# Performer attention and a Fourier-mixing block on one core: keys and queries of 18 of 32 pairs turned by VectorE instead of TensorE, and the other transposes made as row halves

## The chip, the cores and the metric

The kernel runs on one core of a Trainium2 chip. The metric is the device time of one execution in microseconds (us). In the listings PE is TensorE's matmul, PEld its weight load, DVE is VectorE, ACT is ScalarE, POOL is GpSimd, and SP is SyncE, which here only issues DMAs.

## The reference

Two layers follow each other. The first is linear attention by random features (Performer), with B = 8, H = 8, S = 576, D = 64 and 128 features:

```python
scale = 1.0 / np.sqrt(np.sqrt(D))
def phi(x):                                   # x is q * scale or k * scale
    proj = np.einsum('bhsd,md->bhsm', x, omega)
    h = proj - np.sum(x * x, axis=-1, keepdims=True) / 2.0
    return np.exp(h - np.max(h, axis=-1, keepdims=True)) / np.sqrt(m)
kv = np.einsum('bhsm,bhsd->bhmd', k_p, v)     # k_p = phi(k), q_p = phi(q)
z = np.sum(k_p, axis=2)
out = np.einsum('bhsm,bhmd->bhsd', q_p, kv) / (np.einsum('bhsm,bhm->bhs', q_p, z)[..., None] + 1e-06)
```

Its result, with the heads side by side, is x (8, 576, 512). The second layer mixes it by Fourier transforms and applies a two-layer network to each token:

```python
mixed = np.real(np.fft.fft(np.fft.fft(x, axis=1), axis=2))
u = x + mixed
un = (u - mean(u)) / np.sqrt(var(u) + 1e-06)  # over the last axis
return u + np.maximum(un @ w_ch1, 0.0) @ w_ch2
```

w_ch1 is 512 x 2048 and w_ch2 2048 x 512. Both come as 64-bit floats; the kernel reads their two 32-bit words and makes 32-bit floats of them itself. All else is 32-bit float.

## The kernel before, in words

**Pairs.** The attention goes by 32 pairs of heads: pair n is batch n // 4 and two neighbouring heads, with 2 x 576 rows. A load (`loads`, L464) puts nine rows of one head on each of 128 partitions: partition 64 i + p holds rows 9 p to 9 p + 8 of head i, the keys as 9 x 64 numbers, and the queries of the same rows behind them, in one `kq` buffer. There are two such buffers. Keys and queries are one DMA each, in runs of 9 x 64 x 4 = 2,304 bytes; the values (`load_v`) go to buffers of 65 columns a row, in runs of 256 bytes.

The features need keys and queries with the 64 numbers of a head on the partitions. `transposed` (L590) makes that: a buffer's 18 x 64 columns are nine blocks of 128 x 128, and TensorE turns each against an identity (L607) into PSUM. Four blocks fill a bank (2 KB on each of the 128 partitions; there are eight), so the groups are blocks 0 to 3, 4 to 7, and 8. `evicted` (L611) copies each group to `kqT`, on VectorE (L621) or ScalarE (L623). Then `attn` (L668) multiplies by omega (L701: two 64-row matmuls at a time for the first six pairs, four 64 x 64 ones for the others), `softmax` (L637) takes the row maximum (L644, VectorE) and the exponential (L661, ScalarE), L735 makes `kv` with `z` as a 65th column, and a second call of `transposed` turns the query features into `qeT`, in the groups 0, 1 to 4 and 5 to 8, which `evicted` writes in a changed order of rows, two copies for each group. L782 and L790 multiply by kv, and VectorE divides: one reciprocal for each pair (L799, L800) and a multiplication, on VectorE (L811) or ScalarE (L807), which leaves the pair's part of x.

**Mixing.** When the four pairs of a batch are done, `mix` (L823) folds x by the symmetry of the cosine and sine tables (L838 to L874, on VectorE or POOL) and multiplies by the tables. `residual` (L980) then makes u: the cosine part A and the sine part B lie in PSUM; ScalarE copies B to `bmp` (L988), VectorE forms A - B and A + B from it (four products with a scalar, L993, and two sums, L996), x is added, and u goes to DRAM (L1020).

**Network.** The first four tiles of 128 tokens go through an ordinary network in the first part (`plain_norms`, `norm_of`, `plain`), which makes the norm, turns the tile on TensorE (L1172), and multiplies by w1 and w2. Meanwhile `weights` loads the 64-bit weights slab by slab and `narrow` (L522) converts each of 32 slabs: a scaling on ScalarE or POOL (L532), bit operations on VectorE, a product on VectorE (L544) and a sum (L550). The other 4,096 tokens go in eight blocks of 512 through a second part, in which both matrix products use two levels of a Strassen-like scheme (`halves`; L1727, L1878 and L2178 are its matmuls). Its input has to be normed, turned and stored. For twelve tiles of 128 tokens of blocks 1 to 3 that is done ahead, by `ahead` (L1573): four DMAs bring the tile into a borrowed buffer, ScalarE makes the two sums and the norm, POOL the deviation, VectorE turns it by 32 x 32 squares (L1608), and a DMA stores it.

**What sets the order.** All of this is written as Python generators of `Step`s. A step names its engine, or two with a duration each where there is a choice, what must have been made (`after`), and which buffers and PSUM banks it takes and gives ("bank" is one bank, "duo" two neighbouring ones). `Listing.run` (L272) puts the steps in one order, in which the instructions then stand on each engine; nothing reorders them later. The order is recorded: `PICKS` (first part) and `PICKS2` (second part) say for every step which stream comes next and which engine it gets, `BANKS` and `BANKS2` which bank. The twelve tiles ahead are not in these lists. `BETWEEN` and `BETWEEN2` name the points at which the next piece of one is put between listed steps, and `PLACES` the borrowed buffer of each:

```python
PLACES = "kkktttkktuuu"          # k: a kq buffer, t: a kqT/qeT buffer, u: one of its own
...
    if kind == "k":
        place = ld.tile([P, 2 * R, D], F32, name="kq", tag="kq")
```

## Time and profile before

| | |
|---|---|
| median of 3 runs | 1122.09 us (1121.17, 1122.09, 1122.16) |
| the profiled execution, its span from first to last instruction | 1119.2 us |
| instructions in the profile | 31,666, 12,467 of them matmuls and transposes on PE |
| matmul busy time | 1108.4 us of the span |
| VectorE, ScalarE, POOL busy time | 888.7, 539.5 and 390.6 us |
| moved by DMA | 236 MB: 182 read from and 56 written to HBM |

The views that the prediction shows are read in this way. The page's first lines give each engine's busy time with its share of the span and its count. The rows of tenths cut the span in 40 equal slices and give the busy share of each engine in tenths, and the clock that TensorE was granted. The chain of work that ended last is followed back from the last instruction, and its shares are by engine and by line; "banks" stands for all PSUM tiles. A row of a stretch has its start and end, its length, then for PE, PEld, DVE, ACT and POOL the busy time with the number of instructions, then the granted clock, the DMA engines' mean share and GB/s; where a stretch is asked for one line alone, only the engine of that line is listed. A group's row names line, engine, operation, destination and sources, shape and count, then its busy time, the mean of one instruction in ns, and the idle time in front of it with what ended that. A matmul's record holds its latency too, so records overlap.

### The profile page before, as it was taken

The numbers are of one execution on the slowest core, as the hardware profiler recorded it, in microseconds if no ns is written. First come the engines' busy times: TensorE is split into PE (matmuls) and PEld (weight loads), VectorE is DVE, ScalarE is ACT, GpSimd is POOL, SyncE is SP. The second block draws the span as 40 slices with busy tenths as digits, with TensorE's granted clock in tenths as the row PEclk, the third lists the DMA queues.
The fourth block names the chain that finished last, engine by engine and source line by source line (L and its number), as shares of the span: only waits on it lengthen the run. The fifth ranks groups of instructions, "written<-read, shape, count | busy, mean of one in ns | idle before, by whom it ended". The sixth has DMA issues, their size and how long they took to land.

```text
span 1119.2 us, 31666 instructions
## 1 busy us (share of the span) xinstructions
PE 1108.4 (99%) x12467; PEld 1000.4 (89%) x12467; DVE 888.7 (79%) x1685; ACT 539.5 (48%) x1644; POOL 390.6 (35%) x401
## 2 busy tenths in 40 slices
PE   9999999999999999999999999999999999999998
PEld 7888888879868778999999889999889999889998
DVE  6999999987576767687697777888677888568895
ACT  7998898856536455623214452223463223331221
POOL 2443443553563348634413464000365000152000
PEclk9999999999999999999999999999999999999999
DMA  8856766665674669798896778747678656546453
GB/s 243 243 174 188 242 180 191 183 208 176 216 232 156 194 172 343 224 314 262 260 326 224 226 216 248 207 148 238 206 207 261 207 155 216 170 152 220 146 160 105
DMA packets 196549, 236.13 MB, mean 211 GB/s; under 512 B 53808, under 2 KB 120624, under 8 KB 196400
## 3 DMA queue, kind: packets, MB, share of 16 engines
q1 hardware_dynamic: 195904, 233.83, 68.1%
q8 instruction: 99, 1.62, 0.6%
q14 instruction: 50, 0.41, 0.1%
q10 hardware_dynamic: 496, 0.26, 0.1%
HBM read 182.13 MB, written 56.10 MB: 213 GB/s over the span
## 4 chain that ended last, share of the span: by engine, by line
PE 92%; DVE 3%; ACT 2%; DMA 2%; issue 0%; POOL 0%; SPq 0%; DVEq 0%; ACTq 0%
PE banks L2178 31%; PE banks L1727 27%; PE banks L1236 5%; PE banks L701 5%; PE banks L607 5%; PE banks L1259 5%; PE banks L1878 4%; PE banks L735 3%; PE banks L782 2%; PE banks L944 2%; PE banks L894 1%; ACT e L661 1%; DVE nmx L644 1%; PE banks L904 1%; DMA unw<-turned 1%; DMA raw<-in_moe_w_ch_dram 1%
## 5 line engine op out<-in xcount | busy, mean ns | idle before, releaser
L2178 PE MATMUL banks<-wl,sums 128*128 128x128 f32 x1792 | 219.8, 275 | 0.0
L2178 PEld LDWEIGHTS banks<-wl,sums 128*128 128x128 f32 x1792 | 210.6, 192 | 1.0 <-issue 0.3
L661 ACT ACTIVATE e<-banks,nmx 128x128 f32<-128x128 f32 x576 | 165.7, 441 | 23.3 <-DVE nmx L644 22.9
L644 DVE TENSOR_REDUCE nmx<-banks 128x8 f32<-128x1024 f32 (+1 forms) x96 | 89.3, 951 | 16.8 <-PE banks L701 12.4
L2178 PE MATMUL banks<-wl,hid 128*128 128x128 f32 x768 | 99.2, 275 | 0.3 <-DVE part L2154 0.3
L2178 PEld LDWEIGHTS banks<-wl,hid 128*128 128x128 f32 x768 | 92.8, 192 | 1.2 <-DVE part L2154 0.8
L2149 ACT ACTIVATE s<-banks 128x128 f32<-128x128 f32 x112 | 30.9, 277 | 113.6 <-PE banks L2178 103.5
L1727 PE MATMUL banks<-unw,wxw 128*128 128x256 f32 x352 | 85.4, 379 | 0.0
L701 PE MATMUL banks<-om,kqT 64*64 64x128 f32 (+1 forms) x2088 | 79.0, 275 | 1.7 <-ACT kv L751 1.3
L701 PEld LDWEIGHTS banks<-om,kqT 64*64 64x64 f32 (+1 forms) x2088 | 64.5, 138 | 12.7 <-issue 3.2
L2178 PE MATMUL banks<-wl,hx 128*128 128x128 f32 x576 | 74.2, 275 | 0.4 <-DVE part L2154 0.4
L1727 PEld LDWEIGHTS banks<-unw,wxw 128*128 128x128 f32 x352 | 66.6, 190 | 8.9
L1727 PE MATMUL banks<-rx,wxw 128*128 128x256 f32 x288 | 70.8, 379 | 0.0
L2178 PEld LDWEIGHTS banks<-wl,hx 128*128 128x128 f32 x576 | 69.4, 192 | 0.8 <-DVE part L2154 0.6
L1752 ACT ACTIVATE s<-banks 128x512 f32<-128x512 f32 x65 | 38.5, 596 | 65.1 <-PE banks L1727 60.0
L1727 PE MATMUL banks<-ttw,wxw 128*128 128x256 f32 x288 | 69.8, 379 | 0.0
L1236 PE MATMUL banks<-unT,w 128*128 128x128 f32 x512 | 65.4, 279 | 1.7 <-DVE qeT L621 1.7
L550 POOL TENSOR_TENSOR w<-w,raw 128x512 f32<-128x512 f32 x28 | 37.6, 1351 | 77.3 <-DVE raw L544 68.1
L2227 POOL TENSOR_TENSOR more<-more,part 128x512 f32<-128x512 f32 x2 | 2.6, 1315 | 176.6 <-ACT part L2220 176.6
L1236 PEld LDWEIGHTS banks<-unT,w 128*128 128x128 f32 x512 | 60.2, 192 | 4.5 <-issue 2.3
L1727 PEld LDWEIGHTS banks<-rx,wxw 128*128 128x128 f32 x288 | 54.5, 190 | 7.3
L1727 PEld LDWEIGHTS banks<-ttw,wxw 128*128 128x128 f32 x288 | 54.5, 190 | 7.3
(287 smaller groups left out, 2442.3 us busy)
## 6 DMA issues: line engine op xcount, KB each, us to landing
wl<-w2l SPq DMA_DIRECT2D x245, 256.0 KB, 3.9
wxw<-w1x SPq DMA_DIRECT2D x120, 256.0 KB, 3.1
raw<-in_moe_w_ch_dram SPq DMA_DIRECT2D x32, 512.0 KB, 4.8
kq<-in_k_dram SPq DMA_DIRECT2D x32, 288.0 KB, 4.5
kq<-in_q_dram SPq DMA_DIRECT2D x32, 288.0 KB, 4.5
vd<-in_v_dram SPq DMA_DIRECT2D x32, 288.0 KB, 5.4
ur<-us SPq DMA_DIRECT2D x30, 256.0 KB, 5.2
w2l<-sums SPq DMA_DIRECT2D x14, 512.0 KB, 4.9
```

The source lines that it names most:

```text
L550: eng.tensor_tensor(out=dst, in0=dst, in1=lof, op=ALU.add)
L607: nc.tensor.transpose(ps[:, (j - j0) * 128 : (j - j0 + 1) * 128], src(j), ident[:])
L644: nc.vector.tensor_reduce(nmx[:, :, 0:num], pps[:, :, 0 : MF * num].rearrange("p b (c m) -> p b c m", m=MF), axis=AX.X, op=ALU.max, negate ...
L661: nc.scalar.activation(out=e[:, c + (i if num == 1 else 0), :], in_=pps[:, i, MF * c : MF * c + MF], func=AF.Exp, bias=nmx[:, i, c : c + 1],)
L701: nc.tensor.matmul(pps[cols, c, MF * m : MF * m + MF], lhsT=kqT[rows, j, cols], rhs=om2[rows, :],)
L735: nc.tensor.matmul(kvp[cols, i, 0 : D + 1], lhsT=feature(r)[rows, cols], rhs=vds[n % NV][rows, r, :], start=(r == 0), stop=(r == R - 1),)
L1236: nc.tensor.matmul(hp[:, 0:TP], lhsT=w1[:, dc, 128 * fc : 128 * fc + 128], rhs=unTs[key][:, dc, :], start=(dc == 0), stop=(dc == NDC - 1),)
L1259: nc.tensor.matmul(yp[:, 0:DM], lhsT=hs[fc][:, 128 * i : 128 * i + 128], rhs=w2[:, fc, :], start=(fc == 0), stop=(fc == NFC - 1),)
L1727: nc.tensor.matmul(ps[:, span * f : span * f + span].rearrange("f (b q) -> f b q", q=Q), lhsT=left[:, P * f : P * f + P], rhs=right, start ...
L1752: nc.scalar.activation(out=s[:], in_=ps, func=AF.Copy)
L1878: nc.tensor.matmul(cell.rearrange("f t (b q) -> f t b q", q=Q), lhsT=w[:, d, col : col + 128], rhs=right[:, :, d].rearrange("f (t b) q -> ...
L2178: nc.tensor.matmul(ps[:, 0:128], lhsT=left[:, f], rhs=wls[head(j), i, n][:, f], start=start and f == 0, stop=(f == 3), skip_group_check=True,)
```

## The change

**Loads and turns of pairs.** A constant `NTURN = 14` parts the pairs. For pairs 0 to 13, keys and queries are loaded into alternating 64-column places, so that a block of 128 columns holds keys and queries of the same rows; each run of a DMA is 256 bytes. For pairs 14 to 31, `load_blocks` brings keys and queries as squares of 32 x 32 numbers that already stand where they belong, two DMAs each for keys and queries, in runs of 128 bytes. VectorE's transpose, which turns each 32 x 32 square in its place, then makes `kqT` from the buffer in two instructions of 512 and 640 columns. These pairs have no TensorE transposes and no PSUM for `kqT`.

**Row halves.** The other transposes of the pairs, those of omega and those of the four plain tiles are made by `half_turned`: two matmuls on 64 rows each, one on the upper and one on the lower half of the array, each moving 64 columns into a bank of its own. A group then takes two banks and may have five blocks: 0 to 3 and 4 to 8 for `kqT`, 0 to 4 and 5 to 8 for `qeT`. The changed order of rows in `qeT` comes from the identity, which is now loaded from DRAM with a permutation in its other quarters, and from the order in which PSUM is written (`spaced`), so that `evicted` is one plain copy for each group.

**Other parts.** `residual` for all but a batch's last tile has ScalarE prepare A (the odd columns copied, the even ones with B's middle column added or subtracted), and VectorE makes A - B and A + B as two sums of 257 columns. The cosine and sine tables have their columns in order of frequency (even, then odd), and the matmul behind them writes every second column of PSUM. The product in `narrow` may go to POOL, as two instructions. The tiles ahead are listed steps: nine in the first part (`aheads`), three in the second. `wash`, six matmuls that open the second part, gives its banks back after "held". `PICKS` has three digits a step, and the four lists of order and banks are all new.

Counted over the program: 609 transposes of 128 x 128 become 894 of 64 rows; VectorE has 1,611 instructions (1,687 before), ScalarE 1,566 (1,593), POOL 429 (406), SP 1,078 (1,042).

```diff
+    NTURN = 14
     def loads():
         for n in range(B * NP):
             b, pr = divmod(n, NP)
             h = slice(2 * pr, 2 * pr + 2)
-            rows = "i (p r) d -> (i p) r d"
-            yield Step(SP, 0.37, 3.0, take=("kq",), makes=("k", n), kb=288)
+            yield Step(SP, 0.8, 3.6, take=("kq",), makes=("k", n), kb=288)
             kq = ld.tile([P, 2 * R, D], F32, name="kq", tag="kq")
-            nc.sync.dma_start(kq[:, 0:R, :], k[b, h].rearrange(rows, r=R))
             kqs[n] = kq
-            yield Step(SP, 0.47, 3.6, makes=("kq", n), kb=288, bias=-2.98)
-            nc.sync.dma_start(kq[:, R : 2 * R, :], q[b, h].rearrange(rows, r=R))
+            load_blocks(kq, 0, k[b, h], n < NTURN)
+            yield Step(SP, 0.8, 4.0, makes=("kq", n), kb=288, bias=-2.98)
+            load_blocks(kq, 1, q[b, h], n < NTURN)
+
+    def load_blocks(kq, c, src, whole):
+        if whole:
+            nc.sync.dma_start(kq[:, c::2, :], src.rearrange("i (p r) d -> (i p) r d", r=R))
+            return
+        src = src.rearrange("i s d -> (i s) d").rearrange("(a j r) d -> j r a d", j=Q, r=R)
+        dst = kq[:].rearrange("p c d -> p (c d)").rearrange("p (r a i) -> p r a i", r=R, i=Q)
+        for db in range(2):
+            rows = slice(D * c + Q * db, D * c + Q * db + Q)
+            nc.sync.dma_start(dst[rows], src[:, :, :, Q * db : Q * db + Q])
...
-    make_identity(nc, ident[:])
+    for r in range(2):
+        eyes[r, np.arange(D), r, np.arange(D)] = 1.0
+        eyes[r, turn_, 1 - r, np.arange(D)] = 1.0
+    nc.scalar.dma_start(ident[:], nc.inline_tensor(eyes.reshape(128, 128), name="k_eyes").ap())
...
-        yield Step(DVE, 0.61, give=("sign",), port=True, bias=-0.99)
+        step = Step({DVE: 0.61, POOL: 3.0}, give=("sign",), port=True, bias=-0.99)
...
+    def half_turned(to, src, turn=False):
+        for r in range(2):
+            rows, cols = slice(D * r, D * r + D), slice(D * (r ^ turn), D * (r ^ turn) + D)
+            nc.tensor.transpose(to(r), src[rows], ident[rows, cols])
+
+    def spaced(ps, r, at, c):
+        out = ps[:, r, :]
+        return bass.AP(out.tensor, out.offset + at + c, [list(out.ap[0]), [128, 2], [67 - 2 * c, 2], [4, 16]])
+
-    def transposed(src, name, groups, after, makes, give, order=None):
+    def transposed(src, name, groups, after, makes, give, mirror=False):
...
-                0.109 * m,
+                0.062 * m,
+                mode="rows",
                 after=after(j0, j1),
-                take=("bank",) + (("turned",) if j0 == 0 else ()),
+                take=("duo",) + (("turned",) if j0 == 0 else ()),
...
             for j in range(j0, j1):
-                nc.tensor.transpose(ps[:, (j - j0) * 128 : (j - j0 + 1) * 128], src(j), ident[:])
-            yield Fork(evicted(dst, b, j0, j1, makes, order))
+                i = j - j0
+                def to(r):
+                    if not mirror:
+                        return ps[:, r, D * i : D * i + D]
+                    if j == 0:
+                        return ps[:, r, 0:D].rearrange("q (s t) -> q t s", s=2)
+                    c = (j - 1) % 4
+                    return spaced(ps, r, D * (j - c - j0), c)
+                half_turned(to, src(j), mirror and j > 0)
+            yield Fork(evicted(dst, b, j0, j1, makes, mirror))
...
-        for i in range(s):
-            of = ps[:, i, :, ::-1, ::-1] if i and j0 else ps[:, i]
-            copy(dst[:, i], of)
+        if step.eng == DVE:
+            nc.vector.tensor_copy(out=dst, in_=ps)
+        else:
+            nc.scalar.activation(out=dst, in_=ps, func=AF.Copy)
...
+        else:
+            for j0, j1 in ((0, 4), (4, R)):
+                yield Step(
+                    DVE, 0.03 + 0.168 * (j1 - j0), after=(("kq", n),), take=("turned",) if j0 == 0 else (),
+                    give=("kq",) if j0 else (), makes=("kqT", n, j0),
+                )
+                if kqT is None:
+                    kqT = att.tile([128, R, 128], F32, name="kqT", tag="turned")
+                nc.vector.transpose(out=kqT[:, j0:j1, :], in_=flat[:, j0:j1, :])
...
-            ((0, 1), (1, 5), (5, R)),
+            ((0, 5), (5, R)),
...
-                    ab[p1 * n : p1 * n + np_, n, cols],
+                    ab[p1 * n : p1 * n + np_, n, m:KD:2],
...
+        if c < NL:
+            yield Step(ACT, 0.62, take=("bmp",), bias=0.1)
+            bmp, (aa, mi, pl) = taken()
+            nc.scalar.activation(out=mi[:, KD:], in_=pb[:, KD : KD + 1], func=AF.Copy)
+            nc.scalar.activation(out=pl[:, KD:], in_=pb[:, KD : KD + 1], func=AF.Copy, scale=-1.0)
+            nc.scalar.activation(out=aa[:, 1:KD:2], in_=pa[:, 1:KD:2], func=AF.Copy)
+            for k, mid in ((0, mi), (2, pl)):
+                nc.scalar.activation(out=aa[:, k:KD:4], in_=pa[:, k:KD:4], func=AF.Identity, bias=mid[:, KD:])
+            for last, (dst, op) in enumerate(((mi, ALU.subtract), (pl, ALU.add))):
+                yield Step(DVE, 0.34, give=(b0, b1) if last else (), bias=-0.1)
+                nc.vector.tensor_tensor(out=dst[:, 0:KD], in0=aa[:, 0:KD], in1=pb[:, 0:KD], op=op)
...
-    def ahead(j, i):
+    def ahead(j, i, name, pool):
...
+    PLACED = ("kq", "kq", "kq", "turned", "turned", "turned", "kq", "kq", "turned")
+    def aheads():
+        yield Step(NONE, after=tuple(("x", B - 1, pr) for pr in range(NP)))
+        for m, name in enumerate(PLACED):
+            j, i = divmod(m, TB // 128)
+            yield Fork(ahead(1 + j, i, name, ld if name == "kq" else att), 500.0)
...
-        yield Step(NONE, give=(b,))
+        yield Step(NONE, after=("held",), give=(b,))
```

426 lines of the change are left out of this document (255 added, 171 removed).

## The prediction

> **What bounds the kernel now.** I read the page first (engines, tenths, the chain that ended last), then stretches of the span, then the groups of instructions by line and shape, then the DMA rows.
>
> ```profile
> span 1119.2 us, 31666 instructions
> PE 1108.4 (99%) x12467; PEld 1000.4 (89%) x12467; DVE 888.7 (79%) x1685; ACT 539.5 (48%) x1644; POOL 390.6 (35%) x401
> PE   9999999999999999999999999999999999999998
> DVE  6999999987576767687697777888677888568895
> PEclk9999999999999999999999999999999999999999
> ...
> PE 92%; DVE 3%; ACT 2%; DMA 2%; issue 0%; POOL 0%; SPq 0%; DVEq 0%; ACTq 0%
> PE banks L2178 31%; PE banks L1727 27%; PE banks L1236 5%; PE banks L701 5%; PE banks L607 5%; PE banks L1259 5%; PE banks L1878 4%; PE banks L735 3%; PE banks L782 2%; PE banks L944 2%; PE banks L894 1%; ACT e L661 1%; DVE nmx L644 1%; PE banks L904 1%; DMA unw<-turned 1%; DMA raw<-in_moe_w_ch_dram 1%
> ```
>
> The reader is to see that PE is never idle by the record, at full clock (PEclk), and that 92% of the chain is PE. But a matmul's record holds its latency as well as its turn, so "99% busy" leaves room, and DVE stands at 9 tenths in slices 2 to 8. The stretches part the kernel:
>
> ```profile
> 0.00:28.00 28.00, 26.21 (x450) 22.10 (x451) 19.61 (x33) 21.04 (x74) 7.35 (x14) 1.00 0.83 243
> 28.00:235.00 207.00, 204.01 (x4491) 175.37 (x4490) 195.85 (x436) 180.29 (x647) 92.17 (x91) 1.00 0.68 202
> 235.00:373.00 138.00, 136.29 (x2308) 111.02 (x2305) 98.70 (x213) 76.19 (x271) 71.76 (x74) 1.00 0.61 197
> 373.00:420.00 47.00, 47.00 (x291) 33.86 (x290) 33.05 (x85) 23.59 (x63) 14.72 (x29) 1.00 0.60 175
> 420.00:1119.20 699.20, 694.86 (x4936) 658.03 (x4935) 541.48 (x921) 238.38 (x592) 204.64 (x194) 1.00 0.71 218
> ```
>
> Columns: length, busy PE, PEld, DVE, ACT, POOL with counts, clock, DMA share, GB/s. The cuts come from the pairs' divisions, one for each of the 32 pairs of heads (the count in brackets):
>
> ```profile
> 0.00:28.00 28.00, 0.22 (x1) 1.00 0.83 243
> 28.00:235.00 207.00, 4.58 (x22) 1.00 0.68 202
> 235.00:373.00 138.00, 1.92 (x9) 1.00 0.61 197
> ```
>
> So 23 pairs are through at 235 us and the other nine at 373. Up to 235 us DVE works 215.5 of 235 us: 8.4 of its 19.5 idle us lie in the first 28, and from 28 on it is at 95%. There DVE holds the time as much as PE. From 235 to 373 DVE falls to 98.7 of 138 us (72%) while PE stands at 136.3 of 138: this stretch is PE's. From 420 on (the two-level layers) PE works 694.9 of 699.2 us, and the change leaves those matmuls as they are.
>
> **What PE is spared.** All transposes of the pairs stand on one line, 576 of them:
>
> ```profile
> 0.00:28.00 28.00, 8.88 (x54) 5.99 (x54) 1.00 0.83 243
> 28.00:235.00 207.00, 51.97 (x360) 39.55 (x360) 1.00 0.68 202
> 235.00:373.00 138.00, 22.11 (x162) 18.42 (x162) 1.00 0.61 197
> ```
>
> ```profile
> 165.97 1.47 PE L607 MATMUL banks<-ident,kq 128*128 128x128 f32 x12
> 5.41 1.39 PE L701 MATMUL banks<-om,kqT 64*128 64x128 f32 x20
> ```
>
> Twelve in a row take 1.47 us: less the last one's latency of 0.27 us, the row has (1.47 - 0.27) / 11 = 0.109 us for each. The second row shows ten couples of 64-row matmuls in 1.39 us: (1.39 - 0.37) / 9 = 0.113 us for a couple, each moving 128 columns, so two halves of 64 rows run beside each other. The new transposes are such couples, but move 64 columns where these move 128: 0.055 us by that, and I take 0.06. Bounds: 0.055, and 0.109 if a block gains nothing.
>
> - Before: 576 blocks and 33 others (omega, plain norms) at 0.109 = 66.4 us.
> - After: 14 x 9 key-query blocks, 32 x 9 feature blocks and the 33, at 0.06 = 26.8 us. The 162 key-query blocks of pairs 14 to 31 leave PE.
> - PE is spared 39.6 us. Up to the 23rd division (414 blocks before, 126 + 207 after) that is 45.1 - 20.0 = 25.1 us; behind it (162 before, 81 after) 17.7 - 4.9 = 12.8 us; the 33 others give 1.6.
>
> What a page would make of it: the Trainium skill, page "TensorE: Matmul & The Clock Gate", section "LDWEIGHTS (loading the stationary operand)", says that a weight load takes its time from its columns and not from its rows. A half block still loads 128 columns, so by that rule two halves would cost two full loads (128 columns by that section's formula, an estimate: 107 ns each), and the couple would gain nothing even where they overlap; that is a rival below. The loads of this case:
>
> ```profile
> L2178 PEld LDWEIGHTS banks<-wl,sums 128*128 128x128 f32 x1792 | 210.6, 192 | 1.0 <-issue 0.3
> ```
>
> ```profile
> L607 PEld LDWEIGHTS banks<-ident,kq x288: 137/140/224, 3.8 to 339.4; 128*128 128x128 f32 x144
> ```
>
> A transpose's load takes 140 ns where an ordinary one of 128 columns takes 192, so some 50 ns of a load are already missing in this form, which is room enough for a couple in 0.06 us. The trace bears the rule out for ordinary loads only.
>
> **What DVE gets and gives.** From its rows for the first 420 us:
>
> ```profile
> L993 DVE SCALAR_TENSOR_TENSOR bmp<-banks,bmp 128x65 f32<-128x65 f32 x32 | 10.5, 329 | 4.2 <-ACT bmp L988 4.2
> L621 DVE COPY kqT<-banks 128x512 f32<-128x512 f32 x15 | 10.2, 683 | 0.9 <-PE banks L607 0.8
> L996 DVE TENSOR_TENSOR bmp<-banks,bmp 128x128 f32<-128x128 f32 x32 | 9.0, 280 | 0.0
> L621 DVE COPY qeT<-banks 128x256 f32<-128x256 f32 x24 | 8.9, 417 | 6.0 <-PE banks L607 5.9
> L811 DVE TENSOR_TENSOR x<-banks,rden 128x640 f32<-128x640 f32 x28 | 22.8, 822 | 1.6 <-DVE rden L800 0.6 <-DMA vd<-in_v_dram 0.2
> L544 DVE SCALAR_TENSOR_TENSOR raw<-raw,sign 128x512 f32<-128x512 uint32 x32 | 22.0, 687 | 0.6
> L838 DVE TENSOR_TENSOR half<-x 128x1024 f32<-128x1024 f32 x11 | 14.7, 1339 | 0.2
> L1608 DVE STREAM_TRANSPOSE kq<-kq 128x512 f32<-128x512 f32 x5 | 3.5, 706 | 7.0 <-ACT kq L1605 7.0
> ```
>
> - Gone: 27 copies of kqT (15 at 0.683 and 12 short ones at about 0.28: 13.6 us); 40 of qeT (24 at 0.37 by busy time, 16 at 0.21: 12); 64 small pieces of bmp at 0.328 and 32 at 0.28 (30); 8 scalings of x, which go to ACT (6.6); 5 products on raw, to POOL (3.4); 5 sums on half, to POOL (6.7). With ten smaller folds to POOL (5.5): 78 us.
> - Added: 18 turns of 512 columns at 0.706 and 18 of 640 at 0.88, scaled by columns (28.6); 7 kqT and 12 qeT copies of the 512 and 640 sizes at 0.68 to 0.85 (14); 32 bmp sums of 257 columns, between 0.28 (128 columns) and 0.68 (512), taken at 0.42 (13.4); about 40 moved here from POOL and ACT (16 ht, 6 half, 15 of the W2 sums: 17). Together 73 us.
>
> Net -5 us, -3 of it ahead of the 23rd division, where the program's order has DVE do the same 31 conversions of weights in both kernels. DVE gets no relief worth the name where it is full.
>
> **What hides on ACT, POOL and SP.**
>
> ```profile
> L623 ACT ACTIVATE kqT<-banks 128x512 f32<-128x512 f32 x49 | 29.3, 635 | 17.5 <-PE banks L607 17.2
> L623 ACT ACTIVATE qeT<-banks 128x256 f32<-128x256 f32 x104 | 34.4, 444 | 4.1 <-PE banks L607 2.4 <-issue 1.2
> ```
>
> ```profile
> L532 POOL TENSOR_SCALAR w<-raw 128x512 f32<-128x512 f32 x8 | 12.9, 1618 | 19.7 <-DMA raw<-in_moe_w_ch_dram 19.7
> ```
>
> ```profile
> POOL w L550 <- DVE raw L544: 67.1, 17, 9.7
> ```
>
> ACT loses 38 long and 20 short kqT copies and trades 152 small qeT copies for 52 larger ones; it gains 80 scalings, 48 + 32 small bmp pieces and gives 13 weight scalings to POOL: about -14 us of the 301 that the first four stretches add up to. POOL gets those 13 at 1.62 us, five products of about 3 us, ten folds and five sums on half, less 20 others: +35 us on 186. It is hidden by waits such as the 67 us for DVE's product; were that cover gone, the last weight parts would come up to 35 us late. The ordered norms ahead keep their 12 x 5 DMAs on SP; three now stand in the second part. Bounds there: -4 (the idle of 420 on gone) to +9 (a wait like the 1% "unw<-turned" of the chain once more); I take 0, since the matmul order there changes only in its first fifth.
>
> **What the loads cost.** Two stretches in which only one load moves, and the DMA share of the middle:
>
> ```profile
> DMA packets 1127, 0.29 MB, mean 259 GB/s; under 512 B 1127, under 2 KB 1127, under 8 KB 1127
> q1 hardware_dynamic: 1127, 0.29, 117.3%
> ```
>
> ```profile
> DMA packets 132, 0.27 MB, mean 343 GB/s; under 512 B 13, under 2 KB 13, under 8 KB 132
> q1 hardware_dynamic: 132, 0.27, 96.9%
> ```
>
> ```profile
> 140.00:373.00 233.00, 231.29 (x4335) 192.70 (x4334) 189.10 (x420) 157.16 (x560) 115.53 (x119) 1.00 0.62 194
> ```
>
> 1,127 packets of 256 bytes (v) hold 16 engines for 1.173 x 1.1 us: 18.3 ns each. 132 packets, nearly all of 2,304 bytes: 94 ns. So about 9 ns and 0.037 ns a byte.
>
> - Pairs 0 to 13: keys and queries lie side by side in the buffer, 2 x 1,152 packets of 256 bytes in place of 2 x 128: 36.9 us against 21.1 of all 16 engines, +16. In the first 28 us the share is already 0.83, and the first transposes now wait for the query load too. I take +2 us; ends 0 and +10 (all that the first stretches can't hold).
> - Pairs 14 to 31: 4 x 1,152 packets of 128 bytes. No row has that size: at least half a 256-byte packet (9 ns), at most a whole one (18.3) if it saves nothing. By the line above 13.5 ns: 70 us against 27, +43 (ends +20, +68). The stretch from 140 to 373 has 0.62 x 233 = 144 us of DMA; 187 of some 213 us is 0.88. Full, but with two buffers a load has two pairs' time (over 20 us) to land, so 0; at the upper end 9.
>
> **The sum**, against the span of 1119.2: ahead of the 23rd division DVE holds the time, so of PE's 25 us only DVE's own 3 and half of its idle behind the start (11) come through, -3 - 6, and +2 for the first loads: -7 (ends -15, +7). Behind it PE's 13 come through whole (ends -19, if DVE's 72% lets PE also catch up, and 0), the others 1.6. Span 1119.2 - 7 - 13 - 1.6 = 1097.6. The median of 1122.1 stands 2.9 above the span; 1100.5 us.
>
> **The rivals.**
> - *PE's whole gain comes through.* If DVE waited for PE and not the other way round, the early stretch can shrink to DVE's 212.5 and its start of 8, -15, and the late one by 19: 1119 - 36 + 3 = 1086. For it: the chain runs through PE even early. Against: 95% DVE.
> - *The DMA becomes the bound (slower).* A packet of 128 bytes may cost more than one of 256. Place: loads of pairs 14 to 31. At x ns they need 5.18x us; with the 117 us of other traffic the DMA is full once x is 18.5, and the whole gain is gone at (233 + 7 - 117) / 5.18 = 24 ns (the 233 us of before and the 7 won early). At twice the 256-byte price, 36.6, the last pair comes at 140 + 307 = 447 us in place of 373: about 1195 us. For it: no row of a load under 256 bytes. Against: from 2,304 to 256 bytes the price falls evenly. The Trainium skill, page "DMA: Bandwidth & Descriptors", section "Specifications", speaks against the change here: under 512 bytes the engine reads, modifies and writes. The 18.3 ns show no such step at 256 bytes; no run here shows 128.
> - *Half blocks gain nothing* (0.109 each): only the 162 blocks go, 8.8 us early and 8.8 late: 1119 - 3 - 9 + 3 = 1110.
> - *The new order stalls.* Each group of transposes now holds two PSUM banks, not one. If each of the 92 groups waits a third of an eviction's 0.68 us, 21 us go: about 1121, no gain left.
>
> **How the numbers follow.** 0.50 for 1100 (its own range 1090 to 1111), 0.17 for 1086, 0.13 for the DMA, 0.08 for half blocks without gain, 0.12 for stalls. The point is the likeliest case. The range runs from 1082, under the first rival, to 1122, which takes in the stalls and leaves out most of the DMA case. Faster by over 0.2% (what a measurement of this kernel tells from no change: under 1119.8): 0.50 + 0.17 + 0.08 + half of the stalls, 0.81; within 0.2%: 0.05; slower: 0.14.
>
> **What would show it.** Right: couples of 64-row transposes 0.055 to 0.065 us apart; the 23rd division at 225 to 230 us with DVE above 95%, the last at 350 to 356; turns on DVE at 0.70 and 0.88 us; packets of 128 bytes at 13 to 15 ns; from the last division to the end 746 us as before. Wrong if: PE waits on DMA kq in pairs 14 to 31 with the DMA share near 1; couples 0.1 us apart; the early stretch shorter than 222 us, so that DVE was no bound; or PE idle in the second part above 10 us.

## The result and the profile after

The changed kernel takes 1154.26 us (median of 4 runs, 1148.74 to 1158.99) against 1121.63 us: a ratio of 1.0285, 95% interval 1.0253 to 1.0318. It is 32.6 us slower; 1100.5 was predicted. The profiled execution is the slowest of the four: it took 1158.99 us, with a span of 1156.8, so the cuts below show about 5 us more than the medians do.

From the page of the changed kernel (first lines, tenths of PE and its clock):

```profile
span 1156.8 us, 32161 instructions
PE 1093.1 (94%) x12752; PEld 981.4 (85%) x12752; DVE 897.4 (78%) x1609; ACT 530.1 (46%) x1616; POOL 435.0 (38%) x424
...
PE   7899798889999996999989999999999999999998
...
PEclk9999899999999998999999999999999999999999
```

PE works 15 us less than before (1108.4) and the span is 38 us longer: PE now stands idle for 64 us, before for 11. Its row of tenths, nines throughout before, has gaps in slices 1, 2, 5, 7 to 9, 16 and 21, and in slices 5 and 16 the granted clock dips.

The cuts of both kernels, in us: the first, 11th, 23rd and last (32nd) of the pairs' divisions, the matmuls of `wash`, the first product with `tt` and `so` (well into the second part), and the end of the last matmul.

| kernel | 1st | 11th | 23rd | 32nd | wash | tt, so | end |
|---|---|---|---|---|---|---|---|
| before | 21.1 | 110.6 | 235.0 | 373.0 | 417.4 | 427.7 | 1115.5 |
| changed | 26.7 | 115.7 | 249.3 | 376.4 | 434.6 | 453.6 | 1153.2 |
| length of the step, changed less before | +5.6 | -0.5 | +9.2 | -10.9 | +13.8 | +8.7 | +11.8 |

Only the nine late pairs became clearly faster. At the last division the changed kernel is 3.4 us behind; the other 34 us are lost after it. From there to the end of the span it takes 780.4 us, where the prediction said "746 us as before". Seven kernels of the experiments (those of parts 6, 8 and 9) have the same program up to the last pair. In their profiled executions the 23rd division comes at 243.3 to 255.0 us and the last at 370.0 to 378.8, so a difference of a few us at these two marks can be scatter.

The stretches of the changed kernel, with the columns of the prediction's:

```profile
0.00:28.00 28.00, 21.23 (x428) 19.07 (x430) 17.37 (x29) 17.23 (x53) 11.29 (x16) 1.00 0.99 225
28.00:249.00 221.00, 195.56 (x4765) 167.27 (x4760) 199.66 (x381) 175.19 (x620) 128.98 (x113) 0.97 0.80 185
249.00:376.40 127.40, 121.44 (x2291) 98.03 (x2290) 94.42 (x178) 71.40 (x274) 57.32 (x57) 1.00 0.66 163
376.40:434.60 58.20, 53.85 (x321) 34.52 (x320) 48.31 (x103) 26.79 (x79) 23.90 (x38) 1.00 0.77 246
434.60:447.90 13.30, 4.38 (x39) 4.13 (x37) 3.10 (x7) 1.99 (x4) 2.40 (x5) 0.86 0.73 206
447.90:1156.80 708.90, 696.63 (x4920) 658.41 (x4920) 534.58 (x916) 237.46 (x591) 211.07 (x199) 1.00 0.70 213
```

In the early stretch no engine is full: PE 0.88 of the time, DVE 0.90, the DMA engines 0.80. Before, PE had 0.99 and DVE 0.95 there.

The single operations came out as priced. From the order of time, the groups, and the DMA view of a stretch with only 128-byte loads:

```profile
140.78 1.08 PE L713 MATMUL banks<-ident,e 64*128 64x64 f32 x28
```

```profile
L827 DVE STREAM_TRANSPOSE kqT<-kq 128x640 f32<-128x640 f32 x18 | 14.5, 812 | 0.0
L827 DVE STREAM_TRANSPOSE kqT<-kq 128x512 f32<-128x512 f32 x18 | 12.5, 696 | 0.1
```

```profile
DMA packets 750, 0.10 MB, mean 80 GB/s; under 512 B 750, under 2 KB 750, under 8 KB 750
...
q1 hardware_dynamic: 750, 0.10, 50.2%
```

Fourteen couples in 1.08 us, less a latency of some 0.27, are 0.062 us each. The turns take 0.70 and 0.81 us. 750 packets of 128 bytes hold 16 engines for 0.502 x 1.2 us: 12.9 ns each. So the loss is not in the price of any new operation.

### The profile page after: what moved, and what is told of

It reads as the page before. It is cut to its first block, busy times and chain, and to the rows that moved or that the text cites. A ratio compares the mean times of both kernels' runs of the same rounds, so it can differ in the third digit from the quotient of the medians.

```text
span 1156.8 us, 32161 instructions
## 1 busy us (share of the span) xinstructions
PE 1093.1 (94%) x12752; PEld 981.4 (85%) x12752; DVE 897.4 (78%) x1609; ACT 530.1 (46%) x1616; POOL 435.0 (38%) x424
## 4 chain that ended last, share of the span: by engine, by line
PE 55%; DMA 2%; DVE 1%; POOL 0%; issue 0%; ACT 0%; SPq 0%; DVEq 0%
PE banks L2320 29%; PE banks L1869 25%; PE banks L2020 2%; DMA wl<-w2l 2%; DVE sums L1825 0%; DVE hid L1795 0%; DVE rx L1511 0%; POOL hid L1825 0%; DVE tt L1511 0%; POOL rx L1825 0%; POOL so L1825 0%; DVE hid L1825 0%; ACT banks L1901 0%; ACT u L1316 0%; DVE turn L1243 0%
## 5 line engine op out<-in xcount | busy, mean ns | idle before, releaser
L795 ACT ACTIVATE e<-banks,nmx 128x128 f32<-128x128 f32 x576 | 158.8, 411 | 32.3 <-DVE nmx L778 29.1
L846 PE MATMUL banks<-om,kqT 64*64 64x128 f32 (+1 forms) x2088 | 84.2, 282 | 6.9 <-DVE bmp L1157 2.6
L846 PEld LDWEIGHTS banks<-om,kqT 64*64 64x64 f32 (+1 forms) x2088 | 68.1, 142 | 19.8 <-issue 5.8
L1825 POOL TENSOR_TENSOR hid<-hid 128x512 f32<-128x512 f32 x35 | 49.6, 1426 | 37.4 <-DMA w1x<-so 16.5
```

The lines of the kernel that those rows point to most:

```text
L795: nc.scalar.activation(out=e[:, c + (i if num == 1 else 0), :], in_=pps[:, i, MF * c : MF * c + MF], func=AF.Exp, bias=nmx[:, i, c : c + 1],)
L846: nc.tensor.matmul(pps[cols, c, MF * m : MF * m + MF], lhsT=kqT[rows, j, cols], rhs=om2[rows, :],)
L1825: eng.tensor_tensor(out=o, in0=l, in1=r, op=op)
```

## The experiments

Three theories at the start: **P**, the small packets hold the loads up; **N**, the larger number of DMAs and their place in SP's queue do; **O**, the new order of steps loses time by itself, whatever the loads.

**1. Old loads in the changed kernel, new loads in the old one.** `late_rows` gives pairs 14 to 31 the loads of 2,304-byte runs back, `early_rows` pairs 0 to 13, `all_rows` both; `before_new_loads` puts the new loads into the kernel before. What is turned is then other numbers; the work and its order are untouched.

The diff is that of `all_rows`; `early_rows` has the new line in place of the first of the removed ones, `late_rows` behind the `return`.

```diff
     def load_blocks(kq, c, src, whole):
-        if whole:
-            nc.sync.dma_start(kq[:, c::2, :], src.rearrange("i (p r) d -> (i p) r d", r=R))
-            return
+        nc.sync.dma_start(kq[:, R * c : R * c + R, :], src.rearrange("i (p r) d -> (i p) r d", r=R))
+        return
```

`before_new_loads` takes over `load_blocks` and its calls:

```diff
-            nc.sync.dma_start(kq[:, 0:R, :], k[b, h].rearrange(rows, r=R))
+            load_blocks(kq, 0, k[b, h], n < 14)
...
-            nc.sync.dma_start(kq[:, R : 2 * R, :], q[b, h].rearrange(rows, r=R))
+            load_blocks(kq, 1, q[b, h], n < 14)
```

> The changed kernel, but pairs 14 to 31 load keys and queries as whole rows, one DMA each in runs of 2,304 bytes, as the kernel before does; VectorE turns the buffer as in the changed kernel, so that these pairs are computed from numbers in the wrong places (the work is the same, the output is not). Theory A, the loads: SP's queue is busy 20 to 25 of every 28 us with issuing them, transfers come late, TensorE waits, and its clock is halved after the wait; then most of the loss goes: 1128 to 1138 us, the 23rd division at 238 to 243 us in place of 249. Theory B, the new order (two banks for each group, tiles ahead listed late): the loads are covered, so 1149 to 1158 us as the changed kernel, and the 23rd division within 3 us of 249.

> The changed kernel, but pairs 0 to 13 load keys and queries as whole rows in runs of 2,304 bytes; TensorE turns the same blocks of 128 columns, which then hold other rows (the output is wrong for these pairs, the work is the same). Theory A, the loads: the first division comes at 21 to 23 us in place of 27 and the time is 6 to 12 us less than the changed kernel's 1154. Theory B, the order: no more than 5 us less, since what is won at the start is waited away later.

> Both of the above: all 32 pairs are loaded as the kernel before loads them, the rest as in the changed kernel (outputs wrong as said there). Theory A, the loads: 1118 to 1130 us, with the 23rd division at 228 to 236 us and SP's issuing back at some 14 of 28 us. Theory B, the order: 1145 us or more, with the 23rd division at 240 us or later.

> The mirror: the kernel before, with the changed kernel's loads (runs of 256 bytes for pairs 0 to 13, two DMAs each in runs of 128 bytes for the others) and nothing else changed; its transposes then turn numbers from other places (wrong output, same work). Theory A, the loads: slower by 15 to 30 us, 1137 to 1152. Theory B, the order: within 5 us of 1122.

Measured: `late_rows` 1146.84 us (1.0206, 1.0179 to 1.0233), `early_rows` 1148.51 (1.0217, 1.0187 to 1.0247), `all_rows` 1146.36 (1.0211, 1.0188 to 1.0235), `before_new_loads` 1156.35 (1.0296, 1.0270 to 1.0322). `late_rows` and `all_rows` fall between the two times that were forecast for them. With all old loads the changed kernel gains 7.9 us; against the runs of parts 6 and 7, whose edits touch only its start or its changeover (medians 1150.6 to 1152.6), it gains 4 to 6. It is still 23 slower than before, so most of the loss is not the loads (O has a part). The cuts of `all_rows` show where it lies:

| kernel | 1st | 11th | 23rd | 32nd | wash | tt, so | end |
|---|---|---|---|---|---|---|---|
| `all_rows` | 26.4 | 112.5 | 238.7 | 361.1 | 419.0 | 438.2 | 1137.4 |
| length of the step, less before | +5.3 | -3.4 | +1.8 | -15.6 | +13.5 | +8.9 | +11.4 |

With old loads the pairs are through 11.9 us earlier than before, and from the last division to the end 33.8 us are lost, as many as with the new loads. Yet the same loads cost the kernel before 33 us: the order in which the rest stands decides what a load costs. Where it goes there shows in the group of the transposes in `before_new_loads` (first fence, idle time at the end of the row) and in SP's and PE's order of time:

```profile
L616 PE MATMUL banks<-ident,kq 128*128 128x128 f32 x288 | 45.1, 295 | 24.1 <-DMA kq<-in_q_dram 21.0 <-ACT w L543 3.2
```

```profile
140.07 3.73 SPq L483 DMA_DIRECT2D kq<-in_q_dram  x2
```

```profile
147.97 2.15 PE L616 MATMUL banks<-ident,kq 128*128 128x128 f32 x9 [5.95 <-DMA kq<-in_q_dram]
```

From 122.87 to 144.88 us SP issues DMAs almost without a pause. The query load is issued at 140.07 and takes SP 3.7 us, and PE waits 5.95 us for it.

**2. Packets or number?** `before_256` gives the kernel before the alternating places (256-byte packets, the same two DMAs for each pair); `before_four` splits each load by head into two DMAs with the old 2,304-byte runs.

```diff
-            nc.sync.dma_start(kq[:, 0:R, :], k[b, h].rearrange(rows, r=R))
+            nc.sync.dma_start(kq[:, 0::2, :], k[b, h].rearrange(rows, r=R))
...
-            nc.sync.dma_start(kq[:, R : 2 * R, :], q[b, h].rearrange(rows, r=R))
+            nc.sync.dma_start(kq[:, 1::2, :], q[b, h].rearrange(rows, r=R))
```

```diff
-            nc.sync.dma_start(kq[:, 0:R, :], k[b, h].rearrange(rows, r=R))
+            for i in range(2):
+                nc.sync.dma_start(kq[D * i : D * i + D, 0:R, :], k[b, 2 * pr + i].rearrange("(p r) d -> p r d", r=R))
```

> The kernel before with keys and queries of all pairs loaded side by side: as many DMAs (64), but 1,152 packets of 256 bytes each in place of 128 of 2,304; the blocks turned then hold other rows (wrong output, same work). Theory P, SP's issue takes its time by the packets of a DMA and loads come late for it: SP's issue of a load takes 0.55 to 1.0 us in place of 0.4, and the kernel is 8 to 20 us slower than before's 1122. Rival N, the number of DMAs decides: within 4 us of 1122.

> The kernel before with each of its key and query loads cut in two DMAs by head: 128 DMAs in place of 64, packets as before (2,304 bytes); same result. Theory P, packets: within 4 us of 1122. Rival N, the number of DMAs on SP's queue: 8 us slower or more.

Measured: 1138.25 us (1.0133, 1.0118 to 1.0148), about 15 us for the packets, and 1133.41 (1.0099, 1.0079 to 1.0119), about 10 for the number. Both P and N hold in part. The rows of the query loads on SP's own queue show what changed (least, median and largest time of an issue in ns), first of the kernel before, then of `before_256`, `before_four` and the changed kernel:

```profile
L474 SPq DMA_DIRECT2D kq<-in_q_dram x32: 421/432/1784, 1.2 to 312.3; - x32
...
DMA to landing us min/median/max: 3.1/4.5/7.4
```

```profile
L474 SPq DMA_DIRECT2D kq<-in_q_dram x32: 547/1142/1761, 1.5 to 330.3; - x32
```

```profile
L476 SPq DMA_DIRECT2D kq<-in_q_dram x64: 465/596/1790, 2.0 to 322.9; - x64
```

```profile
L583 SPq DMA_DIRECT2D kq<-in_q_dram x36: 582/912/3168, 126.9 to 334.0; - x36
...
DMA to landing us min/median/max: 3.2/4.7/8.8
```

From issue to landing a load takes little more than it took (4.5 us before, 4.7 for half a load in the changed kernel, 5.4 in `before_256`). What grew is the time for which SP is held by issuing: 0.43 us for a query load before, 1.14 with small packets, 2 x 0.60 as two DMAs, 2 x 0.91 in the changed kernel. A key load, issued just ahead of it, grew less with small packets, from 0.36 to 0.58 us. Everything behind it on SP (weights, mixing, stores) is issued later by as much, and SP's order is fixed. The held time alone does not give the loss: all key and query loads together hold SP for 37.0 us before, for 61.5 in `before_256` (15 us lost), for 85.6 in `before_four` (10 lost) and for 104.6 in `before_new_loads` (33 lost). What the small packets cost by their later landing was not parted from it. The Trainium skill, page "Perfetto Trace Analysis", section "DMA Instruction — HWDGE (DVE, Sync)", says that the record of such an instruction covers the wait for the descriptor generator and the generation itself, not the moving of data; the rows agree: the record of 0.43 us ends some 4 us before its load lands.

**3. What is PE's saving worth?** `whole_blocks` turns the first four blocks of each group of the pairs whole, as before, in the same banks; the identity has no permuted quarters, so the order of rows inside `qeT` is not the changed kernel's.

```diff
+                if i < 4:
+                    nc.tensor.transpose(ps[:, i % 2, 128 * (i // 2) : 128 * (i // 2) + 128], src(j), ident[:])
+                else:
+                    half_turned(lambda r: ps[:, r, 256:320], src(j))
+                continue
```

> The changed kernel, but eight of nine of TensorE's transposes for kqT and qeT are whole 128 x 128 blocks against a plain identity, as before, in the same order and banks (the features of the queries then stand in other rows, so the output is wrong; the copies are the same). TensorE has 368 x 0.05 = 18 us more to do, 13 of them ahead of the 23rd division. Theory F, VectorE holds the time there and TensorE's saving was worth nothing: 23rd division within 3 us of the changed kernel's 249, and the whole time up by 0 to 6 us (1152 to 1160). Rival, TensorE holds the time: 1168 us or more, 23rd division at 260 or later.

Measured: 1157.12 us (1.0296, 1.0273 to 1.0320), 3 us more than the changed kernel, with the intervals overlapping. 368 blocks at 0.109 instead of 0.062 us are 17 us of PE's work. PE's busy time between the first and the last division rose by 12.2 us, 9.3 of them ahead of the 23rd. The stretches from the first to the 23rd division, changed first, then `whole_blocks`:

```profile
26.70:249.40 222.70, 197.26 (x4798) 168.64 (x4795) 201.30 (x385) 176.89 (x626) 130.68 (x115) 0.97 0.80 186
28.30:249.30 221.00, 206.53 (x4550) 172.53 (x4549) 202.26 (x384) 176.60 (x625) 131.05 (x117) 1.00 0.82 188
```

The 23rd division comes at 249.3 and the last at 376.4 us in both. The middle of the eight executions with the changed kernel's first part is 248.5 and 374.0, so `whole_blocks` is 1 and 2 us behind for 9.3 and 12.2 us of more work. A scatter of a few us may hide some of it, but hardly all: the early pairs do not get through sooner by most of what PE saves. The same is seen in `all_rows`, where no new load is in the way: from the first to the 23rd division 212.3 us, before 213.9, though PE is busy for 18 us less. For the late pairs, where PE got only 3 us more to do, the run tells nothing.

**4. Is it DVE, then?** `before_pool_products` is meant to relieve DVE in the kernel before: 16 of the 32 products on raw go to POOL, as two instructions each, in the same order.

```diff
+        if i % 2:
+            nc.gpsimd.tensor_scalar(lof, lo, 2.0**-52, None, op0=ALU.mult)
+            nc.gpsimd.tensor_tensor(out=lof, in0=lof, in1=sign[:].bitcast(F32), op=ALU.mult)
+        else:
+            nc.vector.scalar_tensor_tensor(
+                lof, lo, 2.0**-52, sign[:].bitcast(F32), op0=ALU.mult, op1=ALU.mult
+            )
```

> The kernel before with the product on every second weight slab (16 of 32) made by POOL in two instructions, as the changed kernel can do, in place of one on VectorE; same order, same result. VectorE is spared 16 x 0.69 = 11 us, nearly all of it ahead of the 23rd division; POOL gets some 48 us there and was 45% busy. Theory F, VectorE holds the time there: 23rd division 5 to 11 us earlier (224 to 230), 1112 to 1118 us. Rival, no single engine holds it, or POOL's slower conversions come late: within 2 us of 1122, or slower.

Measured: 1138.62 us (1.0141, 1.0123 to 1.0159), 16 us slower; the 23rd division came at 252 us in place of 235. But DVE was not relieved. The stretches from the first to the 23rd division of the kernel before, of `before_pool_products` and of `all_rows`:

```profile
21.10:235.00 213.90, 210.68 (x4622) 181.08 (x4618) 202.68 (x447) 186.91 (x671) 95.22 (x93) 1.00 0.67 199
20.30:251.80 231.50, 216.43 (x4634) 185.25 (x4630) 204.62 (x433) 187.69 (x672) 136.78 (x119) 0.98 0.62 184
26.40:238.70 212.30, 192.46 (x4798) 164.14 (x4797) 201.75 (x384) 176.29 (x626) 132.85 (x119) 1.00 0.67 196
```

DVE is busy for 204.6 us, before for 202.7. The products are gone (16 x 0.687 = 11 us), but other instructions of DVE ran longer beside those of POOL, as its copies of two columns did (before, then `before_pool_products`):

```profile
L840 DVE COPY half<-x 128x2 f32<-128x2 f32 x10 | 1.5, 153 | 0.0
L844 DVE COPY half<-x 128x2 f32<-128x2 f32 x10 | 3.8, 379 | 0.0
```

The waits up to the 23rd division hold this row:

```profile
POOL raw L546 <- DVE sign L542: 52.4, 13, 8.6
```

The new link between DVE and POOL (there is one `sign` buffer) and the longer instructions cost more than the products that left. The run can therefore not tell whether DVE's amount of work holds the early stretch. The third row speaks for it: with old loads the changed kernel takes as long as before, DVE is busy for 0.95 of the time in both, and PE for 0.91 where it was 0.98. No run takes work off DVE alone, so this stays open. With the new loads DVE falls to 0.90 of a longer stretch; which wait makes it longer was not parted further.

**5. The order itself.** `after_free1` and `before_free1` drop the recorded order of the first part and let the planner choose.

```diff
-        picked(PICKS, 3),
-        BANKS,
```

> The changed kernel with the recorded order of the first part taken out: the program's own planner chooses order, engines and banks there by its costs (the second part keeps its record). Theory B, the order recorded for the changed kernel is bad: faster than the changed kernel, 1115 to 1145 us. Rival, the operations themselves are slow in any order: 1150 us or more.

> The kernel before with the recorded order of its first part taken out in the same way, as the yardstick of the run above. An order found by the planner alone should be some 1 to 4% worse than the recorded one: 1133 to 1167 us. If the change's operations are a gain once the record is out of the way, the run above is 5 to 25 us faster than this one; if the new loads decide, it is 5 to 30 us slower.

Measured: 1216.57 us (1.0827, 1.0783 to 1.0870) and 1211.31 (1.0773, 1.0736 to 1.0811). The recorded order is worth 62 us to the changed kernel and 88 to the one before. Under an order tuned for neither, the new operations and loads together bring nothing that can be seen (+5, the intervals overlap).

**6. The changeover.** The changed kernel's only long wait of PE lies between the two parts. SP's, ACT's and PE's order of time there:

```profile
437.86 1.96 SPq L1179 DMA_DIRECT2D us<-x  x2
...
442.37 0.55 SPq L1753 DMA_DIRECT2D turned<-kq  x1
```

```profile
447.30 1.09 ACT L1894 ACTIVATE s<-banks 128x512 f32<-128x512 f32 x2 [10.60 <-DMA turned<-kq]
```

```profile
447.95 3.49 PE L1869 MATMUL banks<-unT,w1s 128*128 128x128 f32 x16 [8.97 <-ACT s L1894]
```

The last tile ahead lies in a `kq` buffer, whose memory the second part uses again. Its store was ready at 437.7 us (DVE's turn ended then), but stands on SP behind loads and stores of the last batch and goes out at 442.37. Until it has landed, ACT may not write `s`, and PE waits 8.97 us. `ahead_idle` leaves out the tiles' work on ACT, POOL and DVE and keeps their loads and stores; `store_by_act` and `last_store_by_act` issue stores of tiles ahead from ACT, the former those of tiles (2, 2) and (2, 3), the latter that of tile (1, 2), the last to go out. The diffs are those of `ahead_idle` (one of its seven instructions, the others alike) and of `last_store_by_act`.

```diff
         yield Step(ACT, 0.65)
-        nc.scalar.activation(out=junk, in_=u, func=AF.Identity, scale=-1.0 / DM, accum_out=mv[:, 0:1])
+        if name == "ur":
+            nc.scalar.activation(out=junk, in_=u, func=AF.Identity, scale=-1.0 / DM, accum_out=mv[:, 0:1])
```

```diff
+        queue = nc.scalar if (j, i) == (1, 2) else nc.sync
-        nc.sync.dma_start(turned_of(j, h)[:, :, k], turn.rearrange("p g d q -> p g (d q)"))
+        queue.dma_start(turned_of(j, h)[:, :, k], turn.rearrange("p g d q -> p g (d q)"))
```

> The changed kernel, but the last two stores of tiles ahead from kq buffers in the first part are issued by ScalarE's queue instead of SP's; same order, same result. Theory C, the changeover: the second part's first copies wait for the last of these stores, because their tiles lie where the kq buffer was; on SP it stands behind two other DMAs (442.4 us, its data ready at 437.7). Issued at about 438.5 it ends the stall of 9 us some 4 to 5 us earlier, TensorE keeps more of its clock, and the 9 us that TensorE idles around 580 to 616 us shrink with it: 1140 to 1149 us. Rival: another transfer holds the second part at the same time, so no more than 2 us less than the changed kernel's 1154.

> The changed kernel, but the nine tiles ahead of the first part are only loaded and stored again: their sums, norms and turns (three instructions on ScalarE, three on POOL, one on VectorE each) are left out, so that blocks 1 to 3 are partly computed from plain rows (wrong output). Theory G, the chain of these tiles sets the start of the second part: the stall of 9 us goes and the time falls by 8 to 15 us, to 1139 to 1146. Rival, their DMAs in SP's order and the last batch's stores set it: no more than 4 us less than 1154.

> The changed kernel, but the store of the tile ahead that is the last in the first part (block 1, tile 2) is issued by ScalarE's queue; same result. Theory C, the changeover: it goes out at about 438.5 us in place of 442.4, the stall of 9 us becomes 4 to 6, and the time 1148 to 1151 us. Rival, another transfer holds the second part: the stall stays above 8 us and the time within 2 us of 1154.

Measured: `store_by_act` 1152.64 us (1.0251, 1.0211 to 1.0292), its last store still on SP and the wait at 7.4; `ahead_idle` 1151.66 (1.0253, 1.0224 to 1.0281), wait 7.9, so the engines' work on the tiles is not the cause; `last_store_by_act` 1150.58 (1.0226, 1.0200 to 1.0252), wait 5.2. In the last one ACT's rows are:

```profile
435.40 0.62 ACTq L1754 DMA_DIRECT2D turned<-kq  x1
...
444.16 1.08 ACT L1895 ACTIVATE s<-banks 128x512 f32<-128x512 f32 x2 [7.51 <-DMA us<-x]
```

The store now goes out at once, and the next in line is what is late: the last batch's own transfers. The wait is 3.8 us shorter, but most of that is lost again: ACT's queue stands at the store until the tile is turned, its next copy starts at 436.07, and PE waits 1.84 us for that copy. From `wash` to the product with `tt` and `so` the kernel takes 18.3 us in place of 19.1. The median is 3.7 us lower, which is less than the scatter of either kernel (1148.74 to 1158.99 and 1145.40 to 1154.03), so a gain by the queue is not shown. The rest of the wait belongs to the batch's being late.

**7. The start.** `warm_first` puts six matmuls that warm the clock ahead of the first transposes.

```diff
     def first():
...
         b, omps = got()
+        for _ in range(6):
+            nc.tensor.matmul(omps[:, 0, 0:128], lhsT=ur1[:, 0:128], rhs=ur1[:, 0:128])
         half_turned(lambda r: omps[:, r, 0:D], om2d)
```

> The changed kernel, but the six warming matmuls stand ahead of the transpose of omega, which waits for the identity's DMA until 4.75 us; same result. Theory D, the identity: the first division comes 2 to 4 us earlier (23 to 25 us in place of 27) and the whole time falls as much, to 1150 to 1152 us. Rival: the transposes of the first pair wait for its loads anyway, so the first division stays within 1 us of 27 and the time within 2 us of 1154.

Measured: 1152.06 us (1.0242, 1.0202 to 1.0282), the first division at 26.4 us. It is 26.4 in `all_rows` too. The changed kernel's first transposes wait for the identity, which now comes by DMA (us in total, times, longest):

```profile
PE banks L713 <- DMA ident<-k_eyes: 4.8, 1, 4.8
```

Each run left the other cause in its place. The transposes of the first pair start at 3.84 us before and at 7.91 in the changed kernel. In `warm_first` they start at 6.49, after a wait of 1.44 us for the query load; in `all_rows`, whose loads are the old ones, at 8.37, behind the identity (5.21) and the warming matmuls. So the identity and the loads cover one another, and no run takes out both.

**8. The second part.** `second_before` gives the changed kernel the old order of the second part (`PICKS2`, `BANKS2` and `BETWEEN2`, with the three last tiles ahead at the old places); `second_and_store` has `last_store_by_act` as well.

```diff
     listing.run(
-        [wash(), late_turns(), late_norms(), halves(), load_leaves(), token_sums(0), w1_sums(), w1_inner(), w1_stored()]
-        + [ahead(3, i, "ur", late) for i in range(1, TB // 128)],
+        [wash(), late_turns(), late_norms(), halves(), load_leaves(), token_sums(0), w1_sums(), w1_inner(), w1_stored()],
         picked(PICKS2, 3),
         BANKS2,
+        betweens(BETWEEN2),
```

> The changed kernel with the second part's order and banks of the kernel before (the three tiles ahead again put between listed steps, the washing banks given back at once); the first part as changed; same result. All runs with the changed second part take 698 to 700 us from its first product with the turned sums to the end, the kernel before 688. Theory E, the second part's own new order costs this: back to 688 us, and 1154 goes to 1141 to 1146 us. Rival, the second part is late because the stall ahead of it (9 us) leaves VectorE behind: it stays at 696 us or more, and 1152 to 1156 us.

> Both of the above: the second part's order of the kernel before, and the last store by ScalarE's queue. Theories C and E together: 1135 to 1141 us; neither: 1152 or more.

Measured: 1144.92 us (1.0187, 1.0158 to 1.0216), -9.3; with the store 1140.90 (1.0159, 1.0142 to 1.0176), -13.4, of which the store's 4.0 are again within the scatter. From the product with `tt` and `so` to the end `second_before` takes 688.6 us, as before (687.8; changed 699.6). SP's order of time at the same point of the program, changed and before:

```profile
578.62 9.24 SPq L1261 DMA_DIRECT2D unw<-turned  x18
```

```profile
531.59 2.69 SPq L1103 DMA_DIRECT2D unw<-turned  x6
534.32 1.37 SPq L2074 DMA_DIRECT2D wl<-w2l  x3
```

and the chain of the changed kernel behind it:

```profile
591.74 5.51 DMA wl<-w2l
...
598.93 5.15 DMA wl<-w2l
...
605.24 7.68 DMA wl<-w2l
```

The new lists issue 18 loads of turned tiles in one lump of 9.2 us; the old ones mix them with the weights. Behind the lump the chain runs through three loads of weights, 18 us of it.

**9. The stretch after the pairs.** PE's order of time behind the last division, before (373.0) and changed (376.4):

```profile
379.50 1.25 PE L894 MATMUL banks<-cs_sb,fold 128*128 128x160 f32 x8
...
385.99 1.25 PE L894 MATMUL banks<-sn_sb,fold 128*128 128x160 f32 x8
```

```profile
378.78 12.28 PE L1412 MATMUL banks<-w,ht 128*128 128x512 f32 x28
...
393.93 1.32 PE L1038 MATMUL banks<-cs_sb,fold 128*128 128x160 f32 x8
...
417.25 1.39 PE L1038 MATMUL banks<-sn_sb,fold 128*128 128x160 f32 x8
```

Before, the last batch's cosine products come 6.5 us after the division and the sine products 13; in the changed order 17.5 and 41, behind matmuls of the plain network. Of the w2 matmuls 57 lie among the late pairs, before 70, and 64 in this stretch, before 47. They hold PE for 25.4 us among the late pairs, before 32.7: 7.3 us of the 11 by which the late pairs became shorter were moved here, not saved. The rows of the stretch from the last division to `wash`, before and changed, and PE's row of waits in the second:

```profile
373.00:417.40 44.40, 44.40 (x268) 31.31 (x267) 32.04 (x83) 22.82 (x61) 14.72 (x29) 1.00 0.59 173
376.40:434.60 58.20, 53.85 (x321) 34.52 (x320) 48.31 (x103) 26.79 (x79) 23.90 (x38) 1.00 0.77 246
```

```profile
PE banks L713 <- DVE u L1326: 4.2, 2, 2.3
```

So the 13.8 us are 9.4 us of work that stood elsewhere before, the w2 matmuls above all (28.4 us against 20.1), and 4.4 us of idle time, nearly all of it two waits of transposes for a normed tile of the plain network. `mix_first` lets the steps of the mixing (stream 6) go ahead of the recorded next step from the last division on, where the planner's clock starts them no later; `mix_first_second` does the same on `second_before`.

```diff
+            hurry = all(("x", 7, pr) in self.made for pr in range(4))
...
+                if path in seen or path not in by or (first and not (hurry and path.split(".")[0] == "6")):
+                    continue
...
+                if got is not None and (first is None or got[0] <= first[0][0]):
+                    first = got, at
```

> The changed kernel with one change of order: once all pairs are divided, the steps of the mixing (folds, products, sums, stores of the last batches) go ahead of the recorded next step wherever the planner's clock lets them start no later; all other steps keep their recorded order, engines and banks; same result. Theory H, the last batch's mixing is late because plain matmuls stand ahead of it on TensorE: its last cosine and sine products end 20 us earlier against the last division (28 us behind it, not 51), the plain matmuls cover its stores, the stall of 9 us goes, and the time falls by 9 to 15 us, to 1139 to 1145. Rival, the second part waits for the tiles ahead, which now come later: no more than 3 us less than 1154, or slower.

> The same, with the second part's order and banks of the kernel before (which alone gave 1145). If the two add up: 1129 to 1136 us. If they are the same loss seen twice: 1141 to 1146.

Measured: 1171.05 us (1.0436, 1.0391 to 1.0480) and 1161.92 (1.0331, 1.0295 to 1.0367): 17 slower each. The 9 us wait between the parts did fall to 1.5, but PE waited 5.1 and 3.2 us for the folds instead, and its clock was halved, as in this stretch:

```profile
393.00:404.00 11.00, 10.11 (x52) 8.10 (x52) 1.75 (x5) 3.28 (x15) 1.32 (x2) 0.50 0.46 170
```

Both forecasts missed. That order is no cure: the stretch from the last division to `wash` became 84 us long, in place of 58.

## Why the prediction was wrong

The step that failed most is what the prediction took for the time behind the last division: 746 us "as before", with 0 for the second part and no term for the way there. It took 780.4 us, and 779.9 in `all_rows`, where the loads are the old ones. The second step that failed is the 0 for the loads of pairs 14 to 31.

- **Prices: right.** Couples 0.062 us (0.06 said, rival 0.109), turns 0.70 and 0.81 (0.70 and 0.88), 128-byte packets 12.9 ns (13.5). POOL's busy time up to the second part rose by 35.5 us (35 said), ACT's fell by 10 (14 said). DVE's rose by 13 where -5 was said: a term mis-sized. Up to the 23rd division it rose by 2 (217.3 against 215.5).
- **No term for the stretch from the last division to the second part: the largest omission**, 22 us (13.8 and 8.7). The prediction read only totals there and did not look at what stands behind the pairs on PE and SP. 9.4 us are work of PE moved there by the new order, 4.4 are idle time, and 9.0 are the wait for the last store and the last batch's transfers.
- **"I take 0" for the second part: wrong.** It is 11.8 us longer behind the product with `tt` and `so`, all but 0.8 of it by its own new order, which costs 9.3 us of the whole. The upper end (+9) was a wait for `unw`; it became one for `wl`. One of the prediction's own signs of being wrong is there: from 447.9 us on PE is idle for 12.3 us.
- **"Full, but with two buffers a load has two pairs' time to land, so 0": wrong step, measured at 4 to 8 us (33 in the old order).** The landing was priced, and that was right (4.7 us). The issue on SP was not priced: twice as many loads, each holding SP twice as long. The rival of the DMA had the place right and the mechanism wrong; the engines' share is 0.80.
- **"PE's 13 come through whole": wrong as it stands.** The stretch of the nine late pairs did shrink by 10.9 us, but 7.3 of them are w2 matmuls moved behind it. With old loads it shrinks by 15.6, and PE is busy for 120.3 of its 122.4 us: there it follows PE's work, as the prediction said, and the new loads take up to 5 us of that back.
- **"Ahead of the 23rd division DVE holds the time ... -7": the sum was wrong, the bound is not refuted.** From the first to the 23rd division it took 8.7 us longer, with DVE at 0.90 and not above 0.95. In `all_rows` it took 1.6 less, with DVE at 0.95 and PE's 18 us of relief without effect, which is what the step said of the two; but half of DVE's idle time (-6) did not go. That PE was 99% busy by the record and carried 92% of the chain did not make its work the bound there.
- **"+2 for the first loads": measured +5.6**, inside its ends, by the identity and the loads, which were not parted.
- **The rival "the new order stalls"** had the sign, at 0.12, and the time, 1121 us, too low. Its mechanism, pairs of banks waiting for evictions, hardly shows: between the first and the last division PE's transposes wait for the copies to `kqT` and `qeT` for 0.7 us, as far as the waits are named.

Of the 32.6 us, 9.3 are shown by the order of the second part and 4 to 8 by the loads; if these add, which was not run, 15 to 19 are left. The rows above show where they lie, at the start and between the last division and the second part, but no run removes them. No version tried beats the kernel before.

## What to carry to other kernels

Where an order is recorded, an engine that is "99% busy" may have slack in each record: add work to it (here 12 us of busy time for 3) before you count on taking work away, and look in the trace whether an edit that should relieve an engine did. Price a DMA by what it holds its issuing queue, packets and number, and list what stands behind it there; the three changes of that kind tried in the kernel before cost it 10 to 33 us. A new order is a change of its own, to be read step by step in the stretches that the edit doesn't touch.
